# A layer kernel's front in another order: fewer changes of TensorE's tile shape, no later warming products, gate and product steps divided between VectorE and GpSimd

## The chip, the cores and the metric

One core of a Trainium2 chip runs the whole kernel. Five engines work at the same time, each through its own queue in order: TensorE (PE) multiplies and transposes, VectorE (DVE), ScalarE (ACT) and GpSimd (POOL) work on vectors, and SyncE (SP) issues the DMA transfers. The metric is the device time of one execution in microseconds, the median of three runs. Less is better.

## The reference

Batch 1, S = 2048 tokens, D = 512 channels, F = 1792. Everything is float32 and the inputs are random. What is computed, cut to its core:

```python
mod = (silu(c) @ w_mod).reshape(1, 6, 1, -1)
sa, ca, ga, sb, cb, gb = (mod[:, i] for i in range(6))
h = layernorm(x) * (1 + ca) + sa                     # x = A_q
k_shift = sum(k_pad[:, t:t+S] * shift_k[:, 3-t] for t in range(4))
kv = k_shift * v
y = causal_long_conv(kv, ssm_k) + kv * ssm_D         # per channel, by FFT
x = x + ga * (h * y)
h = layernorm(x) * (1 + cb) + sb
x = x + gb * ((silu(h @ w_gate) * (h @ w_up)) @ w_down)
```

## The kernel before

The 512 channels make four column groups of 128, numbered 0 to 3. The long convolution is done as transforms, all of them matrix products on PE, with transposes between. For each group: the short convolution of k with four taps (`tap0`, then `tap` three times) gives `u`; `times_v` multiplies it by v into `vt`; `k_turn` and `x_turn` transpose what comes of the filters and of these products on PE (`kt`, `kvt`); `k_first`, `x_first` and `kx_first` do the first step of the transforms (`s`, tile shape 64 x 128) of the filter (`ss`, `er`) and of the data; `swap_x` transposes blocks on DVE (STREAM_TRANSPOSE) in tile X; `x2` and `prod` are the second step and the products of the two spectra (`px` and `pk` on PE, tile shape 64 x 32, then `xs<-pk,xs` on DVE); `inv` is the first step back (`iv`, 32 x 64). Then X is transposed once more: for groups 0 to 2 by a trip through memory (`put`, `get`), for group 3 by DVE again, a second call of `swap_x(12)` to `swap_x(15)`. `y_pe(t, c, ...)` is the last step back (`y`, tile shape 128 x 64) for tile t of 512 tokens (t = 0 to 3) and column groups c.

Beside that run the statistics of the layer norms (`do_stats`: DVE's `bna`, `mva`, then POOL's steps for `rsa`), the modulation (`mod_part`, `mod_bc`, `mod_T`: `pb` and `pm` on PE; `mod_mix` on DVE) and the gate. `gate_n` normalises a tile on ACT into `s`. `gate_p` multiplies half a tile of `s` by one row and adds another (`s<-s,bcs`, two POOL steps of 128 x 1024; there are 16 for the four tiles). `y_gate` multiplies `s` by `y` (DVE). `add_c` and `add_y` add that to x (`x<-x,s`; `add_c` also takes statistics of x, `bnb`). `do_norm2a`, `norm2b`, `norm_t` (`nt` on PE) and `norm_s` (`hraw` on ACT) do the second layer norm; `op_hi` and `op_lo` split its result in two parts for the products of the FFN, `w8_hi`, `w8_lo`, `wd_hi`, `wd_lo` and `split_w` do so with weights (`wg`, `wd`, `wa`, `wsum`). `gu_pe`, `gu_act`, `gu_end` and `downs` are the first FFN products (`g`, `dn`). A loop behind the front does the rest of the FFN; its first PE product is `a`, and `b` reads `wsum`.

What sets the order: the front, from line 1080 on, is a list of calls written out by hand, and the class `InOrder` keeps every engine in the order of that list. A function under `@parts` is called several times for one step: the first call issues the PE part, the next the evacuation on DVE or ACT. All instructions stand at line 63, the helper's, in the profile. Buffers are assigned by the table HOMES, one digit for each tile in the order of creation; `ps` has four PSUM slots of two banks. DMA transfers are issued by SP in the order of the list. `warm(n)` issues n products of the identity by itself, whose result nothing reads: two times 8 at the start, and 6 + 6 ahead of `y_pe(0, 2)`. One PE instruction here has two records in the trace.

PE works with tiles of its array of several shapes: 128 x 128 for transposes, `pm`, `pb` from `part`, and all FFN products, 64 x 128 for `s`, 64 x 32 for `px` and `pk`, 32 x 64 for `iv`, 128 x 64 for `y`, 128 x 32 for `pb` from `wm`. Where one follows another in its row, the tile shape changes.

Of the kernel before, what the change touches and what calls it, by code (L numbers as in the profile page):

```python
# [78 lines left out]
def adaln_h3_swiglu(ctx, tc, q, kT, vT, shk, ssm, dskip, wgu, wdn, c, wmod, e_fwd, e_inv, w_c, out, out_t):  # L79
# [1097 lines left out]
    load_k(2)
    load_v(2)
    mod_load(1, 2)
    prod(1, 2)  # L1180
    load_x(0)
    swap_x(2)
    swap_x(3)
    swap_x(1)
    swap_x(0)
    x2(1, 1)
    x2(1, 1)
# [595 lines left out]
```

## Time and profile before

| | us |
|---|---|
| median of three runs | 593.29 (592.7 to 593.8) |
| the profiled execution | 594.51 |
| its span | 592.7 |
| PE busy in the span | 577.7 (97%) |
| DVE busy | 463.6 (78%) |
| ACT busy | 300.6 (51%) |
| POOL busy | 344.4 (58%) |
| mean granted clock of PE | 0.996 of 2.4 GHz |
| first `a` of the loop, from the span's start | 197.29 |

The front, which the change touches, is the first 197.29 us of the span, a third of it. The busy shares of the whole span are an average over that front and the FFN loop, so they are of little help here; the stretches of the front, and in them the waits of each engine, are to be read one by one. A line of the timeline gives start, length, engine, line, operation, output and inputs, shapes and how many instructions are put together, with the idle time ahead and what ended it in brackets. The matmuls' ends are modelled, so the time from one line's start to the next is the safer measure on PE.

### The profile page before, as it was taken

The page shows a single profiled execution, that of the slowest core. Times are in us where ns is not written, and L with a number is a line of the kernel's source. Part 1 is how long each engine was busy: PE and PEld are TensorE (multiplying, and loading weights), DVE is VectorE, ACT ScalarE, POOL GpSimd, SP SyncE. Part 2 cuts the span into 40 slices and gives each one's busy share as a digit, 9 for nine tenths or more (in the row PEclk, how much of TensorE's full clock was granted, in tenths as well). Part 3 has the DMA queues.
Part 4 walks back from the last instruction along what each step waited for, and adds up shares of the span by engine and source line. Part 5 has one row for each costly group of instructions (what it writes and reads, how often), then busy time and mean ns, then how long its engine had stood idle before and what let it go on. Part 6 is the DMA issues. An engine that isn't in the chain of part 4 may idle for free.

```text
span 592.7 us, 10238 instructions
## 1 busy us (share of the span) xinstructions
PE 577.7 (97%) x4098; PEld 445.5 (75%) x4098; DVE 463.6 (78%) x606; ACT 300.6 (51%) x444; POOL 344.4 (58%) x270
## 2 busy tenths in 40 slices
PE   7999998999989999999999999999999999999997
PEld 6865545443878788888878888888888888888885
DVE  5999998888988877967678877875577777777775
ACT  2897877994375543536436445344433333333330
POOL 0002044987572897694947794476282828374991
PEclk8999999999999999999999999999999999999999
DMA  8978988977321189173746471065343434343403
GB/s 291 417 285 315 282 257 205 369 229 250 146 70 71 36 316 395 68 267 137 236 180 230 161 282 73 1 248 214 125 159 126 159 126 159 125 160 125 160 2 142
DMA packets 41330, 112.56 MB, mean 190 GB/s; under 512 B 3121, under 2 KB 19649, under 8 KB 35778
## 3 DMA queue, kind: packets, MB, share of 16 engines
q1 hardware_dynamic: 41282, 111.90, 53.2%
q8 instruction: 32, 0.52, 0.4%
q14 instruction: 16, 0.13, 0.1%
HBM read 73.61 MB, written 38.28 MB: 189 GB/s over the span
## 4 chain that ended last, share of the span: by engine, by line
PE 81%; DVE 8%; DMA 4%; ACT 2%; POOL 2%; issue 1%; SPq 0%; ACTq 0%; POOLq 0%; DVEq 0%
PE dn L63 13%; PE b L63 12%; PE c L63 11%; PE a L63 11%; PE dq L63 10%; PE d L63 6%; PE g L63 4%; PE s L63 3%; PE y L63 3%; DMA x<-in_q 2%; PE iv L63 2%; DVE xs L63 2%; PE pk L63 1%; DVE bna L63 1%; PE kt L63 1%; PE nt L63 1%
## 5 line engine op out<-in xcount | busy, mean ns | idle before, releaser
L63 PE MATMUL dn<-wd,acts 128*128 128x512 f32 x336 | 83.2, 390 | 0.1
L63 PE MATMUL b<-op,wsum 128*128 128x512 f32 x312 | 79.4, 390 | 0.5 <-POOL wsum L63 0.3
L63 PEld LDWEIGHTS dn<-wd,acts 128*128 128x128 f32 x336 | 62.8, 188 | 13.8 <-DVE sg L63 0.5
L63 PEld LDWEIGHTS b<-op,wsum 128*128 128x128 f32 x312 | 58.4, 188 | 13.4 <-POOL wsum L63 0.8
L63 POOL TENSOR_TENSOR wa<-ws,wa 128x512 fp32r<-128x512 f32 (+1 forms) x28 | 35.2, 1277 | 45.9 <-ACT wa L63 45.9
L63 PE MATMUL a<-op,wa 128*128 128x512 f32 x228 | 58.0, 390 | 0.0
L63 PEld LDWEIGHTS a<-op,wa 128*128 128x128 f32 x228 | 42.6, 188 | 8.8
L63 DVE TENSOR_TENSOR x<-x,dn 128x512 f32<-128x512 f32 x56 | 37.1, 679 | 15.3 <-PE dn L63 15.1
L63 DVE STREAM_TRANSPOSE X<-X 128x1024 f32<-128x1024 f32 x20 | 45.4, 2309 | 3.5 <-ACT X L63 3.5
L63 POOL TENSOR_TENSOR acts<-sg,acts 128x512 fp32r<-128x512 f32 x16 | 23.3, 1467 | 41.7 <-ACT acts L63 41.7
L63 ACT ACTIVATE sg<-sg 128x512 f32<-128x512 f32 x20 | 12.7, 633 | 66.3 <-DVE sg L63 66.3
L63 POOL TENSOR_TENSOR vt<-u,vt 128x512 f32<-128x512 f32 x8 | 10.1, 1294 | 57.6 <-ACT part L63 53.7
L63 POOL TENSOR_TENSOR s<-s,bcs 128x1024 f32<-128x1024 f32 x16 | 38.4, 2419 | 3.1 <-ACT s L63 2.8
L63 PE MATMUL c<-op,wsum 128*128 128x512 f32 x156 | 39.6, 389 | 0.0
L63 PE MATMUL c<-op,wa 128*128 128x512 f32 x156 | 39.6, 389 | 0.0
L63 PE MATMUL d<-op,wsum 128*128 128x512 f32 x156 | 39.6, 389 | 0.0
L63 POOL TENSOR_TENSOR wsum<-sr,wsum 128x1024 fp32r<-128x1024 f32 x14 | 35.6, 2542 | 0.0
L63 PEld LDWEIGHTS c<-op,wsum 128*128 128x128 f32 x156 | 29.3, 188 | 6.1
L63 PEld LDWEIGHTS d<-op,wsum 128*128 128x128 f32 x156 | 29.3, 188 | 6.1
L63 PEld LDWEIGHTS c<-op,wa 128*128 128x128 f32 x156 | 29.3, 188 | 6.1
L63 DVE TENSOR_TENSOR xs<-pk,xs 128x1024 f32<-128x1024 f32 x24 | 28.5, 1214 | 5.5 <-PE pk L63 4.4
L63 DVE TENSOR_TENSOR acc<-acc,dq 128x512 f32<-128x512 f32 x40 | 26.7, 684 | 6.8 <-PE dq L63 6.8
(165 smaller groups left out, 1346.5 us busy)
## 6 DMA issues: line engine op xcount, KB each, us to landing
kept<-wsum SPq DMA_DIRECT2D x12, 1024.0 KB, 8.3
wsum<-kept SPq DMA_DIRECT2D x12, 1024.0 KB, 6.6
kept<-wa SPq DMA_DIRECT2D x12, 768.0 KB, 6.2
wa<-kept SPq DMA_DIRECT2D x12, 768.0 KB, 4.9
ws<-in_wgu SPq DMA_DIRECT2D x16, 512.0 KB, 5.7
wm<-in_wmod SPq DMA_DIRECT2D x6, 1024.0 KB, 8.8
away<-X SPq DMA_DIRECT2D x3, 2048.0 KB, 14.2
X<-away SPq DMA_DIRECT2D x3, 2048.0 KB, 11.5
```

The source lines that it names most:

```text
L63: return lambda *a, **k: self.tc.keep_in_program_order(f(*a, **k))
```

## The change

The list of calls of the front is written in another order, and HOMES follows it. Beyond the order:

- `warm`: 6 products at the start rather than 16, and none ahead of `y_pe(0, 2)`.
- `stats`: the step v + eps moves from POOL to DVE, and -m times rs becomes one DVE step behind POOL's power, in a further part of the function.
- `gate_p` becomes `gate_m` and `gate_a`, with the engine as an argument. Four of the 16 steps are given to DVE: `gate_m(2, 1)`, `gate_a(3, 1)`, `gate_a(2, 0)` and `gate_a(0, 1)`.
- `times_v`: of 16 steps DVE does four (0,2), (0,0), (1,2), (2,1) rather than eight.
- `tap0` of group 0, in two halves, goes from DVE to ACT; those of groups 2 and 3 from ACT to DVE.
- `skip(1)` and `skip(3)` go to POOL, `op_lo("B11")` too; four `add_y`, `w8_lo(1)` and `wd_lo(0)` go from POOL to DVE.
- Transfers: the second half of the first k chunk, the filter parts, c, x and `load_einv` are issued in another order; `put(2)` stands ahead of `mod_load(3, 4)`.

No matrix product of the layer is added or removed. The core of the diff:

```diff
-        pool.tensor_scalar(rs[:, 0, :], v, EPS, None, op0=ALU.add)
+        dve.tensor_scalar(rs[:, 0, :], v, EPS, None, op0=ALU.add)
         pool.tensor_tensor(rs[:, 0, :], rs[:, 0, :], mhalf, op=ALU.pow)
-        pool.tensor_scalar(rs[:, 1, :], m, -1.0, None, op0=ALU.mult)
-        pool.tensor_tensor(rs[:, 1, :], rs[:, 1, :], rs[:, 0, :], op=ALU.mult)
+        yield
+        dve.scalar_tensor_tensor(rs[:, 1, :], m, -1.0, rs[:, 0, :], op0=ALU.mult, op1=ALU.mult)
...
-    @parts
-    def gate_p(t, half):
+    def gate_m(t, half, engine=pool):
         s = S1[t][:, 2 * half : 2 * half + 2]
-        pool.tensor_tensor(s, s, bcs[:, None, 1, :].to_broadcast([P, 2, D]), op=ALU.mult)
-        yield
-        pool.tensor_tensor(s, s, bcs[:, None, 0, :].to_broadcast([P, 2, D]), op=ALU.add)
+        engine.tensor_tensor(s, s, bcs[:, None, 1, :].to_broadcast([P, 2, D]), op=ALU.mult)
+
+    def gate_a(t, half, engine=pool):
+        s = S1[t][:, 2 * half : 2 * half + 2]
+        engine.tensor_tensor(s, s, bcs[:, None, 0, :].to_broadcast([P, 2, D]), op=ALU.add)
...
-    def op_lo(n):
+    def op_lo(n, engine=dve):
         o = BOP[n]
-        dve.tensor_tensor(o[:, 1], held.pop(n), o[:, 0].bitcast(F32), op=ALU.subtract)
+        engine.tensor_tensor(o[:, 1], held.pop(n), o[:, 0].bitcast(F32), op=ALU.subtract)
...
-    def skip(c_):
+    def skip(c_, engine=dve):
         t = SS[c_][0:1, 0, :]
-        dve.tensor_tensor(t, t, dsk[:, c_ * P : (c_ + 1) * P], op=ALU.add)
+        engine.tensor_tensor(t, t, dsk[:, c_ * P : (c_ + 1) * P], op=ALU.add)
...
-    warm(8)
     load_k(0, 0)
-    load_k(0, 1)
+    warm(6)
     load_shk()
-    warm(8)
-    tap0(0, dve, 1)
-    tap(0, 1, 1)
-    tap0(0, dve, 0)
+    tap0(0, act, 0)
...
+    gate_m(3, 1)
+    gate_m(2, 1, dve)
+    gate_a(3, 1, dve)
+    gate_a(0, 0)
+    gate_m(2, 0)
+    gate_m(0, 1)
+    gate_a(2, 0, dve)
+    gate_a(0, 1, dve)
     y_gate(0, 0, 1)
...
-    warm(6)
-    warm(6)
...
+    add_y(3, 0, 4, (0, 1), dve)
+    add_y(3, 0, 4, (2, 3), dve)
```

PE, early, at the first transposes (`kt`, `kvt`, 128 x 128) and first transforms (`s`, 64 x 128). The numbers behind a name tell tiles apart. Before:

```order
L63 MATMUL kt<-ident,kt_129 128x128 x16
L63 MATMUL kvt<-ident,vt_173 128x128 x8
L63 MATMUL kt<-ident,kt_129 128x128 x16
L63 MATMUL s_235<-x_213,er 128x128 x8
L63 MATMUL kvt<-ident,vt_173 128x128 x8
L63 MATMUL s_263<-er,ss_249 128x128 x8
L63 MATMUL s_275<-x_213,er 128x128 x8
L63 MATMUL s_288<-x_261,er 128x128 x8
L63 MATMUL s_301<-x_261,er 128x128 x8
```

In the new order:

```order
L63 MATMUL kt<-ident,kt_129 128x128 x16
L63 MATMUL kvt<-ident,vt_163 128x128 x8
L63 MATMUL kt<-ident,kt_129 128x128 x8
L63 MATMUL kvt<-ident,vt_163 128x128 x8
L63 MATMUL kt<-ident,kt_129 128x128 x8
L63 MATMUL s_245<-x_220,er 128x128 x8
L63 MATMUL s_254<-x_232,er 128x128 x8
L63 MATMUL s_266<-x_232,er 128x128 x8
L63 MATMUL s_290<-x_220,er 128x128 x8
L63 MATMUL s_305<-ss_216,er 128x128 x8
```

The two runs of `kvt` now stand between the `kt` of the same shape, and the `s` follow in one run: no change of shape inside either.

PE, late, behind the last inverse products (`iv`). X_1133 before, and X_1148 after, is the tile of column group 3, X_768 and X_800 that of group 2, the two others those of groups 0 and 1. Before:

```order
L63 MATMUL iv<-xs,wc 64x512 x48
L63 MATMUL pb_1699<-wm,csb 32x512 x4
L63 MATMUL y<-X_244,ei 64x128 x8
L63 MATMUL y<-X_406,ei 64x128 x8
L63 MATMUL pb_1724<-wm,csb 32x512 x4
L63 MATMUL pm<-sel,part_1704 128x1 x4
L63 MATMUL warm<-ident 128x128 x12
L63 MATMUL y<-X_768,ei 64x128 x8
L63 MATMUL pb_1762<-part_844,sel 128x512
L63 MATMUL y<-X_1133,ei_1765 64x128 x8
L63 MATMUL pm<-sel,part_1735 128x1 x4
```

In the new order:

```order
L63 MATMUL iv<-xs,wc 64x512 x48
L63 MATMUL pb_1683<-wm,csb 32x512 x4
L63 MATMUL pb_1692<-wm,csb 32x512 x4
L63 MATMUL pb_1699<-part_737,sel 128x512
L63 MATMUL pm<-sel,part_1688 128x1 x4
L63 MATMUL pm<-sel,part_1697 128x1 x4
L63 MATMUL y<-X_800,ei 64x128 x8
L63 MATMUL y<-X_279,ei 64x128 x8
L63 MATMUL y<-X_437,ei 64x128 x8
L63 MATMUL y<-X_1148,ei_1752 64x128 x8
L63 MATMUL y<-X_800,ei 64x128 x8
L63 MATMUL y<-X_1148,ei_1752 64x128 x8
```

The twelve warming products are gone; both `pb` from `wm`, the `pb` from `part` and both `pm` stand ahead of the first `y`, and two `y` of another tile of tokens stand between the first `y` of group 2 and the first of group 3.

DVE, between the first three second-half transposes of group 3 and the first `y_gate` (`s<-y,s`). Before:

```order
L63 TENSOR_TENSOR xs<-pk,xs 128x1024 x6
L63 STREAM_TRANSPOSE X_1133<-X_1133 128x32x32 x3
L63 TENSOR_TENSOR s_929<-y,s_929 128x2x4x128
L63 TENSOR_TENSOR x_436<-x_436,s_929 128x4x128
L63 BN_STATS bnb_1516<-x_436 128x6
L63 BN_STATS bnb_1518<-x_436 128x6
L63 BN_STATS bnb_1520<-x_436 128x6
L63 BN_STATS bnb_1522<-x_436 128x6
L63 TENSOR_TENSOR xs<-pk,xs 128x1024
```

In the new order:

```order
L63 TENSOR_TENSOR xs<-pk,xs 128x1024 x6
L63 STREAM_TRANSPOSE X_1148<-X_1148 128x32x32 x3
L63 TENSOR_TENSOR s_789<-s_789,bcs 128x1024 x3
L63 TENSOR_TENSOR s_1281<-s_1281,bcs 128x1024
L63 TENSOR_TENSOR s_1281<-y,s_1281 128x2x4x128
L63 TENSOR_TENSOR x_748<-x_748,s_1281 128x4x128
L63 BN_STATS bnb_1529<-x_748 128x6
L63 BN_STATS bnb_1531<-x_748 128x6
L63 BN_STATS bnb_1533<-x_748 128x6
L63 BN_STATS bnb_1535<-x_748 128x6
L63 TENSOR_TENSOR xs<-pk,xs 128x1024
```

The four gate steps (`s<-s,bcs`) now stand ahead of `y_gate`, of the `x<-x,s` and of the `xs` product.

DVE, at the start of the FFN, behind the statistics of the second norm. Before:

```order
L63 TENSOR_TENSOR op<-hraw,op 128x1024
L63 TENSOR_TENSOR s_1261<-y,s_1261 128x2x4x128 x2
L63 TENSOR_TENSOR op<-hraw,op 128x1024
L63 TENSOR_TENSOR s_1261<-y,s_1261 128x2x4x128
L63 TENSOR_TENSOR op<-hraw,op 128x1024
L63 TENSOR_TENSOR hraw<-hraw 128x1024 x2
L63 TENSOR_TENSOR wds<-wds,bcs 128x1024
L63 TENSOR_TENSOR op<-hraw,op 128x1024
L63 TENSOR_TENSOR hraw<-hraw 128x1024
L63 TENSOR_TENSOR sg<-sg,g 128x512 x2
L63 TENSOR_TENSOR op<-hraw,op 128x1024 x2
```

In the new order:

```order
L63 TENSOR_TENSOR s_789<-y,s_789 128x2x4x128
L63 TENSOR_SCALAR rsb_1915<-mvb_1909 128x4
L63 TENSOR_TENSOR s_789<-y,s_789 128x2x4x128
L63 TENSOR_TENSOR wg<-ws,wg 128x1024
L63 SCALAR_TENSOR_TENSOR rsb_1915<-mvb_1909,rsb_1915 128x4
L63 TENSOR_TENSOR op<-hraw,op 128x1024
L63 TENSOR_TENSOR s_789<-y,s_789 128x2x4x128 x2
L63 TENSOR_TENSOR x_450<-x_450,s_789 128x4x256
L63 TENSOR_TENSOR x_285<-x_285,s_789 128x4x256 x2
L63 TENSOR_TENSOR sg<-sg,g 128x512
L63 TENSOR_TENSOR x_450<-x_450,s_789 128x4x256
L63 TENSOR_TENSOR op<-hraw,op 128x1024
```

The four `add_y` (`x<-x,s` 128x4x256) and the low part of `wg` now stand between the `op<-hraw`; the steps for `rsb` stand there as well.

## Rows read from the trace of the kernel before

**Rows 1.** Busy time of each engine in five stretches of the span; column names ahead.

```profile
core 0: us, PE busy (x) PEld busy (x) DVE busy (x) ACT busy (x) POOL busy (x), PEclk, DMA share, GB/s
0.00:16.36 16.36, 10.80 (x96) 10.30 (x97) 10.23 (x16) 5.58 (x9) 0.69 (x6) 0.90 0.90 304
16.36:100.67 84.31, 82.46 (x1159) 51.74 (x1159) 80.22 (x80) 68.92 (x80) 16.03 (x21) 1.00 0.92 294
100.67:152.91 52.24, 50.51 (x772) 24.12 (x770) 42.22 (x35) 37.89 (x47) 45.10 (x22) 1.00 0.83 285
152.91:197.29 44.38, 42.79 (x338) 36.52 (x338) 37.93 (x66) 26.47 (x36) 22.73 (x20) 1.00 0.17 58
197.29:592.70 395.41, 391.12 (x1739) 322.82 (x1737) 293.03 (x412) 161.78 (x273) 259.87 (x203) 1.00 0.44 165
```

**Rows 2.** Waits of PE: for which engine and tile, total us, times, longest.

```profile
PE s L63 <- DMA ss<-in_ssm: 3.0, 1, 3.0
PE pk L63 <- DVE xs L63: 1.7, 2, 1.3
PE nt L63 <- ACT hraw L63: 1.5, 1, 1.5
...
PE b L63 <- POOL wsum L63: 0.3, 1, 0.3
```

**Rows 3.** Timeline of PE before 30 us: start, length, engine, line, operation, count.

```profile
21.11 1.16 PE L63 MATMUL s<-x,er 64*128 64x128 f32 x16
22.20 1.24 PE L63 MATMUL kvt<-ident,vt 128*128 128x128 f32 x8
...
27.05 1.06 PE L63 MATMUL s<-ss,er 64*128 64x128 f32 x16
27.94 1.06 PE L63 MATMUL s<-er,ss 64*128 64x128 f32 x16
```

**Rows 4.** Timeline of PE, 147 to 162 us.

```profile
147.98 2.92 PE L63 MATMUL warm<-ident 128*128 128x128 f32 x24
150.83 1.09 PE L63 MATMUL y<-X,ei 128*64 128x128 f32 x16
151.86 1.13 PE L63 MATMUL pb<-part,sel 128*128 128x512 f32 x2
...
154.92 7.24 PE L63 MATMUL y<-X,ei 128*64 128x128 f32 x128
```

**Rows 5.** Timeline of DVE, at 19 us and from 125 to 153 us.

```profile
19.46 1.28 DVE L63 TENSOR_SCALAR u<-kt,shk_sb 128x2048 f32<-128x2048 f32 x1 [0.72 <-DMA kt<-in_kT]
...
125.03 1.23 DVE L63 TENSOR_TENSOR s<-y,s 128x1024 f32<-128x1024 f32 x1 [2.41 <-PE y L63]
126.29 2.25 DVE L63 TENSOR_TENSOR x<-x,s 128x512 f32<-128x512 f32 x1
...
147.38 4.43 DVE L63 STREAM_TRANSPOSE X<-X 128x1024 f32<-128x1024 f32 x2
...
152.70 0.69 DVE L63 TENSOR_TENSOR x<-x,s 128x512 f32<-128x512 f32 x1
```

**Rows 6.** DVE by line and form, first 198 us: busy us, mean ns, idle before.

```profile
L63 DVE TENSOR_TENSOR op<-hraw,op 128x1024 fp32r<-128x1024 f32 x6 | 10.8, 1804 | 2.7 <-ACT op L63 2.7
L63 DVE TENSOR_TENSOR x<-x,s 128x512 f32<-128x512 f32 x8 | 8.5, 1063 | 0.1
...
L63 DVE TENSOR_TENSOR vt<-u,vt 128x512 f32<-128x512 f32 x8 | 5.0, 687 | 0.1
...
L63 DVE TENSOR_SCALAR u<-kt,shk_sb 128x2048 f32<-128x2048 f32 x1 | 1.3, 1285 | 0.7 <-DMA kt<-in_kT 0.7
...
L63 DVE TENSOR_TENSOR wds<-wds,bcs 128x1024 f32<-128x1024 f32 x1 | 1.2, 1219 | 0.0
...
L63 DVE TENSOR_SCALAR modT<-pm 128x4 f32<-128x4 f32 x2 | 0.2, 150 | 0.0
```

**Rows 7.** Timeline of POOL, at 113 us.

```profile
113.66 14.34 POOL L63 TENSOR_TENSOR s<-s,bcs 128x1024 f32<-128x1024 f32 x6 [1.08 <-ACT s L63]
```

More of the change, by code (lines that the diff above doesn't have):

```diff
@@ L1175, in adaln_h3_swiglu @@
     x_first(1, 1)
-    load_k(3)
[L1177 to L1187, printed above, removed]
+    tap0(2, dve)
+    x_first(1, 2)
+    load_x(2)
+    x_first(1, 2)
+    mod_load(1, 2)
+    x_first(1, 3)
+    x2(0, 2)
+    x2(1, 1)
+    x_first(1, 0)
+    prod(1, 2)
+    x2(0, 2)
+    x_first(1, 3)
+    x2(1, 1)
+    x2(0, 1)
+    x2(0, 1)
+    tap(2, 1)
+    do_stats(3, 1)
+    tap(2, 2)
@@ L1295, in adaln_h3_swiglu @@
-    times_v(3, 1, pool)
-    x2(3, 0)
-    times_v(3, 3, pool)
+    times_v(2, 0, pool)
+    k_turn(1, 3)
+    inv(1)
+    k_turn(1, 3)
+    inv(1)
+    k_turn(1, 0)
+    inv(1)
+    x_turn(2, 0)
+    k_turn(1, 1)
+    times_v(2, 3, pool)
+    times_v(2, 2, pool)
+    x_turn(2, 1)
+    k_turn(1, 0)
+    mod_part(0)
+    k_turn(1, 1)
+    mod_part(5)
+    x_turn(2, 0)
+    do_stats(2, 3)
+    swap_x(7)
+    do_stats(2, 1)
+    do_stats(2, 3)
+    swap_x(4)
+    do_stats(3, 3)
+    do_stats(1, 1)
@@ L1298, in adaln_h3_swiglu @@
+    swap_x(6)
+    mod_part(0)
+    mod_part(5)
+    x2(0, 0)
+    load_x(0)
+    x2(0, 0)
+    tap0(3, dve)
+    tap(3, 1)
+    do_stats(2, 3)
+    x_turn(2, 1)
     x2(3, 2)
     x2(3, 2)
-    times_v(3, 0, pool)
+    prod(0, 2)
+    prod(0, 2)
+    do_stats(3, 3)
+    prod(0, 0)
+    gate_n(2, 0)
+    x_first(2, 2)
+    x_first(2, 2)
+    x_first(2, 3)
+    x_first(2, 3)
+    prod(0, 0)
+    do_stats(1, 2)
+    x_first(2, 1)
+    put_k(2)
+    load_v(3)
+    x_first(2, 0)
+    gate_n(3, 2)
+    x_first(2, 0)
@@ L1301, in adaln_h3_swiglu @@
+    swap_x(5)
+    tap(3, 2)
+    do_stats(1, 3)
+    get_k(2, 2, 3)
+    x_first(2, 1)
+    gate_n(3, 0)
+    inv(0)
+    tap(3, 3)
+    x2(3, 1)
+    inv(0)
+    x2(3, 1)
+    inv(0)
+    x2(3, 0)
+    x2(2, 1)
+    x2(2, 1)
+    prod(3, 2)
+    load_ssm(3)
+    x2(2, 0)
+    gate_n(3, 1)
+    prod(3, 2)
+    do_stats(1, 0)
+    x2(3, 0)
     prod(3, 0)
     prod(3, 0)
-    gate_n(0, 0)
-    x_first(2, 1)
+    x2(2, 0)
+    x2(2, 2)
+    put(0)
+    get_k(2, 0, 1)
+    x2(2, 2)
     prod(3, 1)
-    prod(3, 2)
@@ L1422, in adaln_h3_swiglu @@
     inv(4)
[L1423 removed]
+    k_turn(3, 2)
     k_turn(3, 2)
     inv(4)
[L1426 removed]
     k_turn(3, 1)
+    k_turn(3, 3)
+    k_turn(3, 3)
     k_turn(3, 0)
     k_turn(3, 0)
[L1430 to L1432 removed]
+    k_turn(3, 1)
+    gate_n(1, 0)
+    swap_x(14)
+    swap_x(12)
+    load_einv()
     y_pe(0, 0, 1)
[L1434 to L1437 removed]
+    x2(6, 2)
+    x2(6, 2)
     swap_x(15)
@@ L1494, in adaln_h3_swiglu @@
-    swap_x(15)
-    load_w(0)
-    w8_lo(1, pool)
-    swap_x(14)
+    mod_bc(5)
+    gate_a(2, 1)
+    mod_T(3)
+    mod_T(4)
+    mod_bc(5)
+    swap_x(12)
+    swap_x(13)
+    w8_lo(0, pool)
+    swap_x(14)
+    inv(7)
+    mod_T(3)
+    swap_x(15)
+    y_pe(0, 2)
     y_gate(0, 2)
     add_c(0, 2)
+    y_pe(3, 0, 1)
+    load_einv2()
+    load_w(2)
+    gate_m(1, 1)
+    gate_a(1, 1)
     y_pe(0, 3)
     y_gate(0, 3)
-    gate_p(1, 1)
     add_c(0, 3)
-    gate_p(3, 1)
-    w8_hi(0)
-    gate_p(3, 1)
@@ L1507, in adaln_h3_swiglu @@
-    add_y(2, 0, 4, (0, 1), pool)
-    gate_p(1, 1)
     do_norm2a(0)
     do_norm2a(0)
-    norm2b(0, 1, False)
-    mod_T(3)
-    y_pe(1, 0, 1)
-    y_gate(1, 0, 1)
-    mod_T(3)
-    mod_T(4)
-    w8_lo(0, pool)
-    y_pe(3, 2, 3)
-    y_pe(1, 2, 3)
-    y_pe(3, 0, 1)
-    add_c(1, 1)
-    norm2b(0, 0, False)
+    mod_T(4)
+    y_pe(1, 2, 3)
+    y_gate(1, 2, 3)
+    y_pe(1, 0, 1)
+    do_norm2a(0)
+    y_gate(1, 0, 1)
+    add_c(1, 1)
+    y_pe(3, 2, 3)
+    y_pe(2, 0, 1)
+    norm2b(0, 0, False)
@@ L1527, in adaln_h3_swiglu @@
     norm_s(0, 1)
-    op_hi("B21")
-    y_gate(1, 2, 3)
+    op_lo("B11", pool)
     add_c(1, 3)
-    y_pe(2, 2, 3)
-    load_wd(0)
     add_c(1, 2)
@@ L1606, in norm_rs @@
     def norm_rs(t):
+        next(later[t], None)
         next(later[t], None)
```

562 lines of the change are left out of this document (236 added, 326 removed).

## The prediction

> **What bounds the kernel now.** I read the busy time by stage first [rows 1]. The stages are cut at events on TensorE (PE): 16.36 us is its first transpose of k, 100.67 the first product of the last column group, 152.91 the first gating product (`y`) that reads that group behind its second transposes (`swap_x(12)` to `swap_x(15)`), and 197.29 the first `a` of the steady FFN. The change ends there. Behind it PE is busy 391.12 of 395.41 us, so the change can shift that stage but not shorten it. Ahead of it PE is busy 82.46 of 84.31, 50.51 of 52.24 and 42.79 of 44.38 us: only 1.85, 1.73 and 1.59 us idle. The front is thus paced by PE's own row of matmuls, and taking time out of that row is the right aim. The same rows hold the warning: VectorE (DVE) is busy 80.22 of the 84.31 us, 4.09 us short of being the bound itself; in the next two stages it has 10.02 and 6.45 us free. PE's waits [rows 2] are few: 3.0 us for the first `ss` from DMA, 1.7 for `xs` from DVE, 1.5 for `hraw` from ScalarE (ACT), 0.3 for `wsum` from GpSimd (POOL).
>
> **Changes of tile shape.** Sixteen records of `s` take 27.94 - 27.05 = 0.89 us from start to start where more `s` follow [rows 3]. Where `kvt`, of another shape, follows, the same 16 take 22.20 - 21.11 = 1.09: 0.20 more. A `y` followed by `pb` takes 151.86 - 150.83 = 1.03, and 128 `y` in a row 7.24, that is 0.90 for 16: 0.13 more [rows 4]. I take 0.16 a change, ends 0.13 and 0.20. In the order of PE's instructions I count 55 changes ahead of the first `a` before and 31 after: 34 to 18 ahead of 100.67, and 21 to 13 behind it. All 24 would be 24 x 0.16 = 3.8 us (3.1 to 4.8): 2.6 early, 1.3 late.
>
> **Warming products.** The later 12 last from 147.98 to 150.83 = 2.85 us on PE [rows 4]. They stood where PE would otherwise have waited: the `y` at 152.91 reads a group whose last two transposes on DVE end at 147.38 + 4.43 = 151.81 [rows 5]. Removing them therefore gives only what the transposes let go. In the new order DVE does the four transposes with one tiny `modT` between; before, a `y_gate` of the size of that at 125.03, 1.23 us, stood between the pairs. They would end 1.2 us earlier, at 150.6. PE comes there at about the same time: all that it did ahead of 147.98, 1.3 less, and one `pb`, one `pm` and one `y` more, of 1.0, 1.0 and 0.9 (a `pb` took 152.91 - 151.86 = 1.05; I price a `pm` like it), is 149.6, and a pair of `y` for another tile of rows stands there as well. The `y` that waits starts at 150.6 rather than 152.91, with equally many groups of `y` left and one `pm` fewer: 2.3 + 1.0 = 3.3 us of the 1.3 + 2.85 = 4.15 by which PE's row gets shorter. **-3.3**, ends 0 and -4.15.
>
> **DVE ahead of 100.67.** DVE's second chunk of k starts when its DMA lands (19.46, 0.72 us waited for) [rows 5]. From there on the change gives DVE two more first taps of a whole chunk (2 x 1.285 = 2.57; ACT did those, and now does the two halves that DVE did before 16 us). It takes away two products with v of 0.687 (four of eight go to POOL, two of these from ahead of 19.46), 1.37. It adds about six small statistics steps and removes two `skip`, all near the 0.15 of a `modT`, 4 x 0.15 = 0.6 [rows 6]. The sum is 2.57 - 1.37 + 0.6 = +1.8 us on an engine with 4.09 free, 0.72 of it at a DMA. PE's 2.6 us can therefore not all arrive. Ends: -2.6 (DVE's idle time was all caused by PE) and +1.8 (DVE sets this stage). Between them I take **-0.5**, near the middle: DVE's free time and PE's saving together are still larger than what DVE gets, but DVE has to be ahead of PE at several places, not on average. ACT (68.92 of 84.31) and POOL (16.03) have room for what they are given [rows 1].
>
> **Gating on DVE.** Four of the 16 gate steps leave POOL (six in a row took 14.34, 2.39 each [rows 7]) for DVE, ahead of its first `y_gate` at 125.03, where it waited 2.41 us for PE [rows 5]. A DVE product of that size, both inputs in SBUF, took 1.219 (`wds`) [rows 6]: 4 x 1.219 = 4.9, of which 2.41 fill the wait, so 2.5 us late. Queued behind them on DVE are `y_gate`, two `x<-x,s` and the `xs` products, and PE waits for `xs`, as it did for 1.7 us. Against that, the `x<-x,s` at 126.29 took 2.25 us while POOL's six gate steps ran (113.66 to 128.00), where 152.70 shows 0.69; over all eight the mean is 1.063, so 8 x (1.063 - 0.69) = 3.0 us come back if POOL is done by then [rows 5 to 7]. The term lies between -1.7 (PE's waits vanish) and +4.2 (each gate step lasts as long as one of POOL's, 4 x 2.39 = 9.6, less 2.41 and 3.0). I take **+1.0**: late by 2.5, with half of the 3.0 back. The row of 2.25 shows a two-input DVE step stretched beside POOL's. The Trainium skill, "SBUF — State Buffer", section "Who interferes with whom", says that a DVE instruction with two SBUF inputs contends with a GpSimd instruction that reads SBUF, and that whichever issues later is blocked for the whole instruction; it speaks against dividing one run of gate steps between these two engines. By that rule the term would be its +4.2 end; by the row of `wds` it is +1.0.
>
> **Start of the FFN.** DVE gets four `add_y`, `w8_lo(1)` and `wd_lo(0)` from POOL and gives `op_lo("B11")` away: five more of 1.22 [rows 6], 6.1 us, in a stage in which 6.45 are free [rows 1]. With POOL's `x<-x,s` gone, the `op<-hraw` may fall from their mean of 1.804 to the 1.219 of that size: 6 x 0.585 = 3.5 come back [rows 6]. That leaves 2.6 us, in a stage with room. Behind DVE's added steps stand `op<-hraw` and `hraw`, which PE's `g`, and later `b`, read. The statistics go DVE, POOL, DVE rather than four steps on POOL: two hops between engines for two steps saved, nothing net. Ends: -1.5 (the `nt` wait goes) and +6.1 (none of it covered). I take **+1.0**, the part of 2.6 that falls where PE has no `g` in hand.
>
> **Seam and start.** The second weight's sums stand earlier on POOL, so `b`'s wait goes [rows 2]: **-0.3**. At the start the first `s` needs less data (-1.0 at most, since the taps and DVE's second chunk at 19.46 stay where they are), but ten fewer warming products may leave `s` at a lower clock: the granted clock is 0.90 of 2.4 GHz over the first 16.36 us [rows 1]; the first 64 `s` would take 4 x 0.89 = 3.6 us at that level and 7.1 at 1.2 GHz, so at most 3.6 more. All bytes ahead of the second chunk are still sent: **0**, ends -1.0 and +3.6. The later transfers (`put(2)` now ahead of two weight loads on SP's queue, `load_einv` behind `get(1)`) I cost at nothing: no wait of PE for an X from DMA is among those listed [rows 2]. If one comes back late, PE waits at `y` for that long.
>
> **Sum.** 0 - 0.5 - 3.3 + 1.0 + 1.0 - 0.3 = -2.1 us. The profiled execution took 594.51 us, 592.7 of it span; there the changed kernel would take 592.4. The median of the three runs is 593.29, 1.2 us below the profiled one, and from it I forecast 593.29 - 2.1 = 591.2.
>
> **Rivals.** (a) PE is the bound everywhere and DVE fits: all changes of shape, the warming products and the seam count, 3.8 + 2.85 + 0.3 = 6.95, so 586.3. For it: PE has almost no idle time now. Against: DVE's 80.22 of 84.31, and the transposes that end at 151.81. (b) The gate steps on DVE and POOL hold each other up: that term is +4.2 instead of +1.0, so 594.4, hardly another time than before. For it: 2.25 against 0.69 us. Against: POOL's run is shorter by four steps and may be over. This is what the skill's rule above would give. (c) Slower: DVE becomes the bound from the first `y` of the last group to the first `a`. If the `op<-hraw` stay near 1.8 us because POOL's other work stretches them as well, and DVE's 6.45 free us are waits for PE and ACT that stay, nothing covers the 6.1 us; +6.1 instead of +1.0 gives 596.3. It decides from about 4 us uncovered. (d) The list does no more than move the waits: PE's shorter row meets DVE at each stage, and only the seam remains, 593.0.
>
> **How the numbers follow.** Forecast 0.42, (a) 0.12, (b) 0.10, (c) 0.24, (d) 0.12. A measurement of this kernel tells about 0.2% (1.2 us) from no change. Faster: (a) and 0.36 of the forecast, 0.48. Same: (d), 0.06 of the forecast and most of (b), 0.26. Slower: (c) and a little of (b), 0.26. The range goes from (a), 586.3, to just above (c), 597.0, and leaves out the cases in which two ends fall together.
>
> **What would show it.** In the changed profile: the first `px` of the last group at about 100.2 (98 says that DVE kept up, 102 that it did not); four DVE gate rows near 1.2 us, not 2.4; the first `y` of the last group at about 150 with a short PE wait for X; `op<-hraw` near 1.2 us; the first `a` at about 195.2, and no wait at `b`. I am wrong if the start loses more than 2 us to clock or DMA, if a transfer of X comes back late at `y`, or if the FFN from the first `a` on leaves its own length of 395.4.

## The result and the profile after

| | before | after |
|---|---|---|
| median, us | 592.84 (17 runs, 592.56 to 594.40) | 596.06 (17 runs, 593.76 to 598.06) |
| the profiled execution | 594.51 | 597.2 |
| its span | 592.7 | 595.2 |
| mean granted clock in it | 0.996 | 0.994 |

The changed kernel is slower: ratio 1.0047, 95% interval 1.0035 to 1.006. The forecast was 591.2, faster. The measured median lies inside the range that was given, on the other side of the kernel before.

The stages of the changed kernel, cut at the same events as in [rows 1] and once more at the first `nt` (157.89); columns are stretch, length, then busy time of PE, PE's weight loads, DVE, ACT and POOL, granted clock, DMA share, GB/s:

```profile
0.00:16.70 16.70, 9.61 (x77) 8.86 (x77) 9.59 (x15) 7.60 (x12) 1.41 (x7) 1.00 0.88 302
16.70:99.98 83.28, 79.38 (x1142) 50.93 (x1143) 81.02 (x80) 66.83 (x81) 20.13 (x18) 1.00 0.91 296
99.98:149.09 49.11, 48.19 (x771) 24.66 (x771) 46.85 (x41) 35.81 (x45) 32.77 (x14) 1.00 0.86 304
149.09:157.89 8.80, 8.34 (x145) 7.80 (x145) 8.56 (x25) 2.43 (x4) 1.02 (x1) 1.00 0.14 55
157.89:199.32 41.43, 36.47 (x186) 29.67 (x185) 33.34 (x51) 23.43 (x32) 15.65 (x13) 0.92 0.18 64
199.32:595.20 395.88, 391.32 (x1739) 322.84 (x1737) 295.89 (x418) 161.08 (x273) 250.82 (x193) 1.00 0.44 164
```

Event by event, from the two profiled executions:

| stretch ends at | before, us | after, us | length after less before |
|---|---|---|---|
| first `kt` | 16.36 | 16.70 | +0.34 |
| first `px` of the last group | 100.67 | 99.98 | -1.03 |
| first `nt` | 162.09 | 157.89 | -3.51 |
| first `a` of the loop | 197.29 | 199.32 | +6.23 |
| end of the span | 592.7 | 595.2 | +0.47 |
| sum | | | +2.50 |

So the change wins 4.5 us between the first `kt` and the first `nt`, and loses 6.2 us in the stretch behind it, which was 35 us long. The waits of PE that answer to [rows 2] (engine and tile, total us, times, longest):

```profile
PE s L63 <- DMA er<-in_e_fwd: 4.3, 1, 4.3
PE px L63 <- DVE X L63: 2.3, 2, 1.6
PE nt L63 <- ACT hraw L63: 1.6, 1, 1.6
PE y L63 <- ACT hraw L63: 1.5, 1, 1.5
PE dn L63 <- DVE sg L63: 1.5, 1, 1.5
```

Those of `pk` for `xs` (1.7) and of `b` for `wsum` are gone; new are those of `px`, for DVE's transposed X, and of `y` and `dn`, these two in the stretch that got longer. That stretch on PE:

```profile
149.09 4.70 PE L63 MATMUL y<-X,ei 128*64 128x128 f32 x80 [0.21 <-issue]
...
157.89 1.32 PE L63 MATMUL nt<-ident,n 128*128 128x128 f32 x8
160.81 1.73 PE L63 MATMUL nt<-ident,n 128*128 128x128 f32 x8 [1.60 <-ACT hraw L63]
164.08 3.68 PE L63 MATMUL y<-X,ei 128*64 128x128 f32 x32 [1.54 <-ACT hraw L63]
167.69 8.57 PE L63 MATMUL g<-op,wg 128*128 128x512 f32 x36
...
192.16 1.52 PE L63 MATMUL dn<-wd,acts 128*128 128x512 f32 x6
195.16 4.33 PE L63 MATMUL dn<-wd,acts 128*128 128x512 f32 x18 [1.47 <-DVE sg L63]
199.32 1.52 PE L63 MATMUL a<-op,wa 128*128 128x512 f32 x6
```

The same stretch in the kernel before, from the second `nt` on:

```profile
164.88 1.09 PE L63 MATMUL nt<-ident,n 128*128 128x128 f32 x8 [1.54 <-ACT hraw L63]
165.91 1.97 PE L63 MATMUL y<-X,ei 128*64 128x128 f32 x32
167.81 5.74 PE L63 MATMUL g<-op,wg 128*128 128x512 f32 x24
...
191.50 5.95 PE L63 MATMUL dn<-wd,acts 128*128 128x512 f32 x24
197.29 1.52 PE L63 MATMUL a<-op,wa 128*128 128x512 f32 x6
```

The second `nt` starts 2.92 us behind the first, against 164.88 - 162.09 = 2.79 before. From there to the next `y` it is 3.27 us, against 1.03: 1.54 of waiting for `hraw`, and the eight `nt` themselves take 1.73 instead of 1.09. The 32 `y` take 3.61 us to the first `g`, against 1.90. The `g` with the `nt` among them take 24.47 against 23.69, and from the first `dn` to `a` it is 7.16 against 5.79, 1.47 of it a wait for `sg`. Granted clock (third column from the end) in the same stretch:

```profile
160.00:162.00 2.00, 1.19 (x7) 1.19 (x8) 1.93 (x7) 1.80 (x3) 0.09 (x1) 0.78 0.00 0
162.00:164.00 2.00, 0.54 (x3) 0.14 (x1) 2.00 (x9) 1.42 (x3) 2.00 (x1) 0.50 0.14 23
164.00:166.00 2.00, 1.92 (x18) 1.93 (x20) 2.00 (x4) 1.90 (x3) 1.27 (x2) 0.50 0.68 240
166.00:168.00 2.00, 2.00 (x19) 1.67 (x16) 2.00 (x4) 1.27 (x2) 1.30 (x1) 0.52 0.00 0
```

From about 161 to 168 us PE runs at 0.50, the 1.2 GHz level. An estimate of what that costs here comes from the `nt` and the `y` at either level: (1.73 - 1.09) + (3.61 - 1.90) = 2.35 us. Ahead of the fall PE had waited 1.60 us, with short waits of 0.21 and 0.46 in the ten us before. In the kernel before, PE waited as long at the same place, behind 14 us and more without a gap, and kept 1.00.

### The profile page after: what moved, and what is told of

Read it like the earlier page. It is cut to its first block, busy times and chain, and to the rows that moved or that the text cites. A ratio compares the mean times of both kernels' runs of the same rounds, so it can differ in the third digit from the quotient of the medians.

```text
span 595.2 us, 10149 instructions
## 1 busy us (share of the span) xinstructions
PE 573.3 (96%) x4054; PEld 444.8 (75%) x4054; DVE 475.2 (80%) x625; ACT 297.2 (50%) x444; POOL 321.8 (54%) x243
## 4 chain that ended last, share of the span: by engine, by line
PE 84%; DVE 10%; ACT 2%; issue 2%; DMA 1%; SPq 0%; ACTq 0%; DVEq 0%
PE dn L63 14%; PE b L63 12%; PE a L63 12%; PE c L63 12%; PE dq L63 10%; PE d L63 6%; PE s L63 4%; DVE X L63 4%; PE px L63 3%; PE g L63 3%; PE pk L63 2%; DVE xs L63 2%; PE y L63 2%; PE iv L63 1%; PE kt L63 1%
## 5 line engine op out<-in xcount | busy, mean ns | idle before, releaser
L63 POOL TENSOR_TENSOR vt<-u,vt 128x512 f32<-128x512 f32 x12 | 17.0, 1443 | 46.4 <-DVE u L63 38.0
L63 POOL TENSOR_TENSOR s<-s,bcs 128x1024 f32<-128x1024 f32 x12 | 28.5, 2395 | 15.5 <-ACT s L63 15.3
L63 DVE SCALAR_TENSOR_TENSOR u<-kt,shk_sb,u 128x1024 f32<-128x1024 f32 (+6 forms) x15 | 28.7, 1916 | 6.0 <-ACT u L63 5.7
L63 ACT COPY p<-a 128x512 f32<-128x512 f32 x26 | 15.4, 591 | 33.3 <-PE a L63 33.3
```

The lines of the kernel that those rows point to most:

```text
L63: return lambda *a, **k: self.tc.keep_in_program_order(f(*a, **k))
```

## The experiments

Each median below stands beside runs of the kernel before on the same chip; a difference in us from the changed kernel is the difference of the two ratios times 593. The changed kernel's ratio is 1.0047.

**One function back in the FFN loop.** `stats` also serves token tiles 2 and 3, whose steps run inside the FFN loop. Columns of the next two fences are those of [rows 5]. DVE, in the changed kernel:

```profile
257.95 0.69 DVE L63 SCALAR_TENSOR_TENSOR rsb<-mvb,rsb 128x4 f32<-128x4 f32 x1 [1.13 <-POOL rsb L63]
```

PE at the same time:

```profile
261.17 0.51 PE L63 MATMUL dn<-wd,acts 128*128 128x512 f32 x1 [0.59 <-ACT acts L63]
261.90 0.73 PE L63 MATMUL dn<-wd,acts 128*128 128x512 f32 x2 [0.22 <-DVE acts L63]
```

DVE's step on `rsb` waits 1.13 us for POOL's power, the steps behind it in DVE's queue come late, and PE waits 0.59 and 0.22 for `acts`. Two runs took this part by itself. The first puts the old form back for these two tiles in the changed kernel:

```diff
+        if name in ("b2", "b3"):
+            pool.tensor_scalar(rs[:, 0, :], v, EPS, None, op0=ALU.add)
+            pool.tensor_tensor(rs[:, 0, :], rs[:, 0, :], mhalf, op=ALU.pow)
+            pool.tensor_scalar(rs[:, 1, :], m, -1.0, None, op0=ALU.mult)
+            pool.tensor_tensor(rs[:, 1, :], rs[:, 1, :], rs[:, 0, :], op=ALU.mult)
+            to[name] = rs
+            return
```

> The changed kernel with one function put back for the two later token tiles alone: their statistics run as four steps on POOL again, as before the change; the front keeps the new form. Theory (the new form leaves a DVE step waiting 1.13 us for POOL's power inside the FFN loop, and PE's dn waits behind it near 260 us): PE's offset against the kernel before no longer grows from 1.4 to 2.5 us there, 1.1 us less than the changed kernel, about 595.0. Rival (the loop only passes on what it inherits from the front): the time stays at 596.1 and dn still waits at 260 us.

Measured: 594.71 (ratio 1.0027, 1.0015 to 1.0038), 1.2 us less than the changed kernel. From the first `a` to the end it takes 394.99 us instead of 395.88, and no wait of `dn` in the loop is listed. The second gives the kernel before the new form for these two tiles, and nothing else:

```diff
+        late = name in ("b2", "b3")
+        (dve if late else pool).tensor_scalar(rs[:, 0, :], v, EPS, None, op0=ALU.add)
         pool.tensor_tensor(rs[:, 0, :], rs[:, 0, :], mhalf, op=ALU.pow)
+        if late:
+            yield
+            dve.scalar_tensor_tensor(rs[:, 1, :], m, -1.0, rs[:, 0, :], op0=ALU.mult, op1=ALU.mult)
```

> The kernel before with one part of the change alone: the new form of the statistics for the two later token tiles, whose steps run inside the FFN loop. Theory: DVE waits about 1.1 us for POOL's power near 258 us and PE's dn behind it, so 1.0 to 1.2 us slower than before. Rival (this cost came only from the changed kernel's offset): no difference.

Measured: 594.23 against 593.15 (1.0017, 1.0008 to 1.0025), 1.0 us slower; from `a` to the end 396.54 us instead of 395.41, and PE's waits of 0.6 and 0.2 us for `acts` at `dn` appear. Both agree: this part of the change costs 1.0 to 1.2 us (0.5 to 1.5 by the second run's interval), shown in both directions.

**The slot of the last `y`.** In the changed kernel one PSUM slot serves the first `nt`, the second `nt` and then the last `y`, because the three other slots hold `y` that DVE has not yet taken.

```diff
-    y_gate(2, 0, 1)
     do_norm2a(1)
...
+    y_gate(2, 0, 1)
     add_c(1, 3)
...
-  ps  ...221302201
+  ps  ...212301102
```

(The digits show the end of the table row: slots 1 and 2 exchanged behind the two `nt`.)

> The changed kernel with y_gate(2, 0, 1) called ahead of add_c(1, 3) and the last y of the front put into the PSUM slot that this frees (slots 1 and 2 exchanged from there to the end of the front). Theory (this y waits 1.54 us for hraw only since it shares one slot with both nt; that idle time and the one ahead of it also lower PE's clock from 161 to 167.5 us, 2.4 us of cost): the wait at y goes, the first g starts 1.5 us earlier with the clock still low and up to 3.4 us earlier with it high, so 592.7 to 594.6. Rival (DVE's added work sets the start of the FFN): y starts earlier but the first a does not, and the time is 596 to 597 because the statistics of tile 1 come 1.2 us later.

Measured: 594.6 (1.0022, 1.0013 to 1.0031), 1.5 us less than the changed kernel, the smallest gain that was expected. PE in this run:

```profile
161.40 1.97 PE L63 MATMUL y<-X,ei 128*64 128x128 f32 x32
163.30 3.41 PE L63 MATMUL g<-op,wg 128*128 128x512 f32 x12
168.36 5.74 PE L63 MATMUL g<-op,wg 128*128 128x512 f32 x24 [1.65 <-DVE wg L63]
```

The wait at `y` is gone, in this execution the clock stays at 1.00, and `g` starts 5.84 us behind the first `nt` instead of 9.80. But from `g` to `dn` it takes 26.70 us instead of 24.47, 1.65 of it one wait for `wg`: DVE's `w8_lo(1)`, given to it by the change, is next to be late. So of the 3.96 us that came free, 2.23 are lost again ahead of `dn`, and 0.65 are won at `dn`. The rival was half right. That the moved step also keeps the clock up is not shown: the eleven runs have mean clocks from 0.99 to 1.0, and the run with all three edits, below, has the same step and a low clock at this place.

**The slot of the fourth `g`.**

```diff
-  ps  ...21302201
+  ps  ...21302231
```

> The changed kernel with two PSUM slots exchanged late in the front: the fourth g in slot 3 rather than 0. Theory (the second dn waits 1.47 us because the first bank of the FFN's pool lies on the slot in which the fourth g still waits for DVE's sg): this wait goes, the first a is 1.5 us earlier, 594.6. Rival (DVE's sg is late since DVE has too much to do, whatever the slot): a later dn waits for it instead, less than 0.5 us gained.

Measured: 596.58 (1.005, 1.0035 to 1.0064), no gain. The wait of `dn` for `sg` stayed, 1.47 us. A likely reason, not shown: the slots are first used in the order 2, 3, 1, 0, and if their banks lie in that order, the pool of the FFN begins on slot 2, where the third `g` lies, and not on slot 0. In the run with the moved `y_gate`, above, and in the next one, which have the third `g` in slot 1, the wait for `sg` is absent, and `dn` waits 0.78 us for DVE's `x` instead; that fits, but was not tried alone.

**The three edits together.**

```diff
-  ps  ...221302201
+  ps  ...212301132
```

(With these digits go the `stats` lines and the moved `y_gate` from above.)

> All three edits together in the changed kernel. If the three costs are separate they add: 1.1 + 1.5 to 3.4 + 1.5 us less than the changed kernel, 590.1 to 592.0, which is faster than the kernel before (592.8). If DVE's work is the bound the front ends where it did and the time is about 595.

Measured: 593.79 against 593.43 (1.0002, 0.9993 to 1.0012): the time of the kernel before, 2.7 us less than the changed kernel. That is the 1.2 and the 1.5 us of the first two edits, and the 590.1 to 592.0 that was expected did not come. PE, where the changed kernel loses its time:

```profile
161.04 1.72 PE L63 MATMUL nt<-ident,n 128*128 128x128 f32 x8 [1.60 <-ACT hraw L63]
162.68 2.96 PE L63 MATMUL y<-X,ei 128*64 128x128 f32 x32
```

The wait at `y` is gone, but behind the one wait of 1.60 us PE runs at 0.50 from about 161 to 165 us. In the same execution a DVE step is late. POOL, then DVE:

```profile
162.14 2.35 POOL L63 TENSOR_TENSOR op<-hraw,op 128x1024 fp32r<-128x1024 f32 x1 [6.68 <-ACT op L63]
```

```profile
162.47 2.57 DVE L63 TENSOR_TENSOR x<-x,s 128x512 f32<-128x512 f32 x1
```

An `x<-x,s` of DVE takes 2.57 us instead of 0.69, to 0.55 us behind the end of POOL's `op_lo("B11")`.

**POOL steps beside DVE's chain.** Four further versions start from the first two of these edits, three of them with the first `dn` in slot 3 (digits ...212301103), and move one or a few steps. The rows of HOMES that follow from that are left out below. The first makes the second weight's parts early, `w8_lo(1)` on POOL:

```diff
+    load_w(1)
+    w8_hi(1)
+    w8_lo(1, pool)
     norm2b(0, 0, False)
...
-    w8_lo(1, dve)
```

> The run with the three edits, and two more: the second weight's parts (load_w(1), w8_hi(1), w8_lo(1)) are made ahead of the first nt, with w8_lo(1) on POOL, which is idle there, and the first dn is put into slot 3. Theory (with the slot freed, PE waits next for DVE's w8_lo(1), 0.4 to 1.7 us, and the second dn 0.8 us for the bank of the first): both waits go, 1.2 to 2.0 us less than the run with the three edits, about 592. Rival (the rest of DVE's queue is as late): g waits for another DVE step, under 0.5 us gained.

The second does so too, takes `op_lo("B11")` to DVE, and puts the last `y` between the two `nt`, with the gate step that makes its slot free ahead of it:

```diff
+    y_gate(3, 0, 1)
...
+    y_pe(2, 2, 3)
...
-    op_lo("B11", pool)
+    op_lo("B11")
...
-    y_pe(2, 2, 3)
-    y_gate(3, 0, 1)
```

> As the run before in this call, and the last y (32 products) now stands between the two nt, in the slot that y_gate(3, 0, 1), called earlier, has freed; op_lo of B11 is on DVE. Theory (the 1.6 us in which PE waits for hraw between the nt are idle only for want of a free slot, and PE's clock falls there): PE is busy there, the clock stays at 1.0 from 158 to 168 us in the profile, and the time is 1.5 to 3 us less than the run with the three edits, 590.5 to 592.3, faster than the kernel before. Rival (DVE is the bound as soon as PE waits less): g waits for op or hraw as long as nt waited before, and the time is 592.5 to 594.

Measured: 594.67 (1.0025, 1.0012 to 1.0037) and 594.31 (1.0019, 1.0009 to 1.0028), no gain over the three edits alone, where both theories expected one; the first is slower as far as the intervals tell, for the second they overlap. The waits for `wg` did go, but the first `nt` came later: PE waited 0.9 us for DVE's `s` and twice 0.4 for `n`. In both, POOL's step of 2.37 us now lay beside DVE's step on `rsb` for the first norm (157.50 and 157.56 us in the first run), and that step took 2.32 us instead of 0.16; the two `y_gate` around it kept their 1.21. In the second run the place between the two `nt` was filled as planned, and the clock still fell (0.53 from 161 to 164 us): with the first `nt` late and torn, PE had idle time there all the same. So this run leaves open what a filled hole would do for the clock. The last two take POOL's step away from DVE's chain, and then put another one beside it:

```diff
-    op_lo("B11", pool)
     add_c(1, 3)
+    op_lo("B11")
     add_c(1, 2)
```

> The run with the three edits, with op_lo of B11 on DVE instead of POOL (called between add_c(1, 3) and add_c(1, 2)) and the first dn in slot 3. Theory (in the run with the three edits an x<-x,s of DVE took 2.57 us instead of 0.69 while POOL made this op_lo, so POOL's step costs DVE 1.9 us where DVE itself would need 1.2, and g has to wait for the low part): the statistics of tile 1 come 0.7 us earlier, g's 0.4 to 0.6 us and dn's 0.8 us of waiting go, 592.0 to 593.0, at or below the kernel before. Rival (DVE's queue is the bound whoever does this step): 593.5 to 594.5.

```diff
-    w8_lo(1, dve)
+    w8_lo(1, pool)
```

> The same with w8_lo(1) on POOL. If DVE's load is what counts, 0.5 to 1.2 us less than the run before in this call; if a POOL step of 2.4 us beside DVE's chain of x<-x,s stretches that chain, 0.5 to 2 us more.

Measured: 593.48 against 593.48 (1.0004, 0.9992 to 1.0015) and 596.08 (1.0042, 1.0029 to 1.0055). The first is as fast as the kernel before and as the three edits, no more, about as its rival said: `g` has to wait for `wg` for 2.40 us in its profile, and behind that the clock is at 0.50 from about 171 to 175 us:

```profile
169.59 7.34 PE L63 MATMUL g<-op,wg 128*128 128x512 f32 x24 [2.40 <-DVE wg L63]
```

The second loses 2.3 us against the first for one step of POOL, and its rows show how. POOL, then DVE:

```profile
167.88 2.34 POOL L63 TENSOR_TENSOR wg<-ws,wg 128x1024 fp32r<-128x1024 f32 x1
```

```profile
167.94 2.29 DVE L63 SCALAR_TENSOR_TENSOR rsb<-mvb,rsb 128x4 f32<-128x4 f32 x1
```

A DVE step on four numbers per partition, 0.16 us elsewhere, takes 2.29 us and ends with POOL's `wg` beside it. On it hang `n` of the second norm and, in DVE's queue, `op<-hraw` and `g`, which waits 3.5 us.

The profiled executions of the first three of these four versions took 598.15, 595.78 and 595.27, that is 1.5 to 3.5 us more than their medians. Their rows show where waits lie, not what the median lost.

**Parts of the change undone.** The gate steps:

```diff
-    gate_m(2, 1, dve)   gate_a(3, 1, dve)   gate_a(2, 0, dve)   gate_a(0, 1, dve)
+    gate_m(2, 1)        gate_a(3, 1)        gate_a(2, 0)        gate_a(0, 1)
```

> The changed kernel with all 16 gate steps on POOL. Theory (the four steps on DVE are a gain, since they take 1.64 us each there and fill a wait): POOL needs 4 x 2.4 = 9.7 us more behind 122.2, so the first y_gate starts near 132 instead of 126.8, PE waits for xs behind it, and the time is 598 to 600. Rival (dividing the run costs time by contention): the time falls to 594 or 595.

Measured: 602.05 (1.0156, 1.0136 to 1.0175), 6.5 us more than the changed kernel and more than the 598 to 600 expected. PE waits where it did not in the changed kernel:

```profile
132.44 1.36 PE L63 MATMUL px<-X,wc 64*32 64x512 f32 x16 [2.77 <-DVE s L63]
135.19 1.96 PE L63 MATMUL pk<-K,wc 64*32 64x512 f32 x16 [1.39 <-DVE xs L63]
```

From about 133 to 140 us, behind the first of these waits, the clock is at 0.50 as well, so the 6.5 us are waits and clock together. At the two `nt` PE has the waits of the changed kernel, 1.60 and 1.54 us, and here the clock stays at 1.00.

The work at the start of the FFN:

```diff
-    op_lo("B11", pool)   w8_lo(1, dve)    wd_lo(0, dve)    add_y(..., dve)  (4 times)
+    op_lo("B11")         w8_lo(1, pool)   wd_lo(0, pool)   add_y(..., pool) (4 times)
```

> The changed kernel with the work at the start of the FFN back where it was: four add_y, w8_lo(1) and wd_lo(0) on POOL, op_lo of B11 on DVE. Theory (the slots, the clock and the statistics in the loop cost the time, not DVE's 6.1 us): the waits of 1.6 and 1.5 us around nt stay, the first a moves by less than 1 us either way, the time is 595.5 to 597. Rival (DVE's added work sets the start of the FFN): the first a is 3 to 5 us earlier and the time 591 to 593.

Measured: 607.4 (1.0229, 1.0211 to 1.0246), 10.8 us more than the changed kernel, far outside both expectations. PE's waits there:

```profile
PE dn L63 <- DVE sg L63: 3.4, 1, 3.4
PE g L63 <- DVE rsb L63: 2.5, 1, 2.5
...
PE g L63 <- DVE op L63: 1.6, 1, 1.6
```

DVE's steps are held up beside POOL's (one `hraw` took 3.43 us, the next 1.21), and the clock was at 0.50 in three stretches of about 4 us, from 163, 170 and 204 us on. So in this order both divisions of work are gains against the same work on POOL, large ones. That DVE's added steps cost nothing does not follow: with the `y` slot freed, `g` waits for one of them.

**The later warming products.** Taken from the kernel before, alone:

```diff
-    warm(6)
-    warm(6)
     y_pe(0, 2)
```

> The kernel before without the 12 later warming products, nothing else changed. Theory (they stand where PE would wait for the last transposes, and do nothing for the clock, since PE is full for 14 us behind them): the y of group 3 starts when its transposes end, 151.8 instead of 152.9, so 0 to 1.1 us faster than before, with the same spread of the mean clock (0.996 to 1.0). Rival (they keep the clock up for the stretch behind them): runs with a mean clock of 0.99 to 0.995 appear, and the median is 1 to 3 us slower than before.

Measured: 596.1 against 593.36 (1.0044, 1.0032 to 1.0056), 2.6 us slower, as the rival said. PE, and the clock of one stretch behind:

```profile
151.65 1.09 PE L63 MATMUL y<-X,ei 128*64 128x128 f32 x16 [1.99 <-DMA ei<-in_e_inv]
...
153.66 8.87 PE L63 MATMUL y<-X,ei 128*64 128x128 f32 x128
```

```profile
155.00:158.00 3.00, 3.00 (x36) 3.00 (x35) 2.12 (x9) 0.85 (x1) 1.51 (x4) 0.58 0.00 0
```

PE waits for a DMA, `ei`, issued at 146.66 us here and at 147.20 before, and the `y` behind it starts at 151.65 (152.91 before). The last transpose, which the same `y` needs, ends at 151.23, so it alone would have held PE to about 0.4 us ahead of that. Behind that wait of 1.99 us it runs at 0.58 on the mean of 3 us, and the 128 `y` last 8.87 us instead of 7.24. All five runs have a mean clock of 0.99 to 0.994. The products' results are read by nothing; what they were worth was to keep the clock up through a wait. Put back into the changed kernel:

```diff
+    warm(6)
+    warm(6)
     y_pe(0, 2)
```

> The changed kernel with the 12 warming products put back ahead of y_pe(0, 2). Theory (the clock falls because of the two idle times around nt, not for want of the products 12 us earlier): PE's row gets 2.85 us longer ahead of nt, the DVE chain from y with it, the clock falls as often as in the changed kernel, and the time is 598 to 599. Rival (the products keep the clock up): mean clock 0.998 to 1.0 in most runs, and the 2.85 us are paid back by some 2.5, so about 596 or below.

Measured: 600.34 (1.0092, 1.0064 to 1.0119), by the ratios 2.7 us more than the changed kernel, from 1.0 to 4.3 by this run's interval; its six runs go from 595.23 to 600.7.

```profile
147.36 2.92 PE L63 MATMUL warm<-ident 128*128 128x128 f32 x24
150.22 10.70 PE L63 MATMUL y<-X,ei 128*64 128x128 f32 x192
...
166.35 3.68 PE L63 MATMUL y<-X,ei 128*64 128x128 f32 x32 [1.54 <-ACT hraw L63]
```

The products last 2.86 us, but PE's short waits of 0.21 and 0.46 us behind them are gone: from the start of `pm` to the first `nt` it is 15.19 us instead of 13.62, 1.57 more. PE is then without a gap from 147.36 to the first `nt`, and after the two waits the clock is down all the same (the 32 `y` take 3.61 us again). In the changed order the `ei` transfer is issued at 143.44 rather than 147.20 and nothing waits for it, so there is no such wait for the products to stand in. This speaks against the idea that the short waits ahead of `nt` are needed for the clock to fall. The waits around `nt` were enough here; with the gate steps on POOL, above, the same two waits were not followed by a fall.

## Why the prediction was wrong, point by point

- **Changes of shape: right.** PE's busy time from the first `kt` to 99.98 fell from 82.46 to 79.38, 3.08 us. Of that, 0.89 is one `k_first` (16 records of `s`), which the new order puts behind this cut: 48 records of `s<-er,ss` stand there instead of 32. That leaves 2.19 us for 16 changes, 0.14 each, at the lower end of 0.13 to 0.20.
- **DVE ahead of 100: right in kind.** The stretch got 1.03 us shorter (I took 0.5), 0.89 of it by the `k_first` that left; of the 2.19 us hardly 0.2 arrived. PE's idle time rose from 1.85 to 3.90; the longest wait, 1.6 us, is for DVE's transposed X, and DVE is busy 81.02 of 83.28.
- **Warming products and last transposes: right in size, half right in reason.** The `y` of the last group starts at 149.09, where I gave 150.6. I had named the transposes alone as what the `y` at 152.91 needs; the run without the products shows that the `ei` transfer comes 0.4 us later still. The term came out because the new order also issues that transfer 3.8 us earlier, at 143.44, which I had priced at nothing. I had also priced the products by their time alone, and their worth before was the clock.
- **Gating on DVE: better than the forecast.** The four steps, and the `y_gate` behind them:

```profile
120.10 6.57 DVE L63 TENSOR_TENSOR s<-s,bcs 128x1024 f32<-128x1024 f32 x4
126.77 1.22 DVE L63 TENSOR_TENSOR s<-y,s 128x1024 f32<-128x1024 f32 x1
128.03 0.69 DVE L63 TENSOR_TENSOR x<-x,s 128x512 f32<-128x512 f32 x1
```

  Taken one by one, the first took 3.16 us and the other three 1.21 each: POOL's own run of gate steps ended at 122.18, and only the first met it. The `y_gate` starts at 126.77 instead of 125.03, as estimated to within 1 us. The `x<-x,s` take 0.69 rather than 2.25, PE's wait of 1.7 for `xs` at `pk` is gone, and the last transpose ends at 148.99. From 100 us to the first `nt` the two terms together were to give -2.3; they gave -3.5, with the 0.89 us of the `k_first` to carry.
- **Start of the FFN: here the prediction failed.** The term was +1.0, and measured it is +6.23. The reasoning "2.6 us of DVE work are left, in a stage with room" was sound as far as it went: the row of `op<-hraw` fell to 1.217, as forecast.

```profile
L63 DVE TENSOR_TENSOR op<-hraw,op 128x1024 fp32r<-128x1024 f32 x5 | 6.1, 1217 | 1.0 <-ACT op L63 1.0
```

  What it left out is that PE comes to `nt` 4.2 us early and that everything from there on is a chain across three engines (DVE's statistics, ACT's `n`, PE's `nt`, ACT's `hraw`), in which PE has nothing else to do. DVE itself shows no gap from 140.1 to 174.0 us. The early arrival turned into a wait for a PSUM slot (1.54), a low clock (2.35), a wait at `dn` for a slot that DVE still had to empty (1.47, of which 1.37 remain against before) and 0.8 more among the `g`. The slot is shown by the run that moves one `y_gate`. The low clock is measured, but what brings it about is open, since it falls at the same place with that step moved too (the three edits). That behind the slot a step of DVE is waited for next, `wg`, is shown by the run with the moved `y_gate` and by the first of the two that take `op_lo("B11")` to DVE. The wait at `dn` is measured and its slot not shown. I had bounded the term by DVE's work, and an end of +6.1 was in the list; that 6.23 lies beside it is luck, since 2.35 of it is clock.
- **Seam: right.** `b` does not wait, and with the old statistics the loop takes 394.99 against 395.41: -0.4.
- **The loop: missed.** "The change can shift that stage but not shorten it" forgot that it can lengthen it: the function `stats` and `norm_rs` behind the list are in the diff, and I costed them for the front alone, at "two hops between engines for two steps saved, nothing net". In the loop the hop makes DVE's queue wait 1.13 us: +1.0 to 1.2 us.
- **Start: right.** +0.34, with the granted clock at 1.00 there in this profile and 0.90 in the one before. Between executions the first `kt` of all these kernels moves from 15.6 to 17.6 us.

Of the rivals, (c) gave the time, 596.3, but not by its sum: `op<-hraw` did not stay at 1.8, and 2.35 us of the stretch are clock and about 1 us of the loss lies in the loop. Its other half, that DVE becomes the bound behind the last group's `y`, is borne out in part by DVE's row without a gap and by the wait for `wg`; with the work back on POOL the kernel is 10.8 us slower still. (b) is seen on one of the four steps (3.16 instead of 1.21 us), but not at its price: without the gates on DVE the kernel takes 6.5 us more. (a) fails at PE's waits for DVE. (d), that the waits only move, describes the front up to 100 us, where PE's time saved became idle time. In the sum of the profiled executions: +0.34 - 1.03 - 3.51 + 6.23 + 0.47 = +2.50 against -2.1.

What stays open: why the clock falls in one execution and not in another at the same wait. The mean clock of the changed kernel's 17 runs goes from 0.988 to 1.0. The slowest has the lowest (598.06 at 0.988) and the two fastest have 1.0, but one run at 0.999 took 597.04, and among the runs with the three edits the four fastest have 0.997 to 0.999, so the clock alone does not order the times. The three runs of the changed kernel at 1.0 took 593.76 to 594.82, and those of the kernel before at 1.0, beside the first four experiments, 592.64 to 593.5: about 1 us of the loss is there with the clock up. No version tried here beats the kernel before beyond the uncertainty.

## What to carry to other kernels

Time won on a busy engine is worth only what the chain behind it lets through: follow the new, earlier arrival to the next place where that engine depends on others, and ask which buffer it will need there and who empties it. When a helper function changes, cost it at every place that calls it, not only where the diff is large. Products that do nothing may hold the clock through a wait; before removing them, find the wait that they stand in.
